# One 128-row tile transposed by TensorE instead of by DMA, two tile loads moved, ten more small products

## The chip, the core and the metric

The kernel runs on one core of a Trainium2 chip. TensorE (PE in the profile; PEld is its weight loads) multiplies, VectorE (DVE), ScalarE (ACT) and GpSimd (POOL) do the elementwise work, and SyncE (SP) issues every DMA of the kernel from one queue. The metric is the device time of one execution in microseconds (us); lower is better.

## The reference, cut to what matters

```python
x = A_x                                   # 1 x 2048 x 640, bf16
xn = layernorm(x)                         # no gain, no bias
# A: 32 heads of 20; phi(u) = [softmax(u w_phi), softmax(-u w_phi)]
q, k, v = split(xn @ wqkv)
kv = phi(k)^T v;  z = sum_s phi(k);  num = phi(q) kv;  den = phi(q) z
a = (num / (den + 1e-6)) @ wo
# B: gated unit, F = 1536
b = (silu(xn @ w1) * (xn @ w3)) @ w2
return x + a + b
```

## The kernel before

The 2048 rows of x are 16 tiles of 128 rows. A tile is loaded with its rows on the partitions (buffer `xin`, printed by the profile as `reg_h`), VectorE and ScalarE work out mean and variance (`ln_stats`, `ln_root`, or `stats` on GpSimd for later tiles), `lx` normalises it in place (line 289), and it is then transposed into `xnT`, which holds the 640 features in five chunks of 128 partitions and all 2048 rows as columns. Every product reads `xnT`. There are two ways to transpose a tile: `by_dma(t)` (line 759) is one DMA transpose issued by SP, and `by_pe(dst, t, ps)` (lines 294 to 304) is five 128x128 transposes on TensorE into the PSUM bank `ps` and two copies by ScalarE, of two and three chunks, into `dst`.

All engines run through one order that is written out by hand, and each of them takes its instructions strictly in that order. The part that the change touches is the opening, lines 764 to 841:

- Tiles 0, 1 and 2 are also transposed before normalisation (`by_pe(xrT, ...)`), so that their products with the v weights (`raw_part`, line 308) can begin while the statistics are made; `raw_scaled` (lines 320 and 325) then multiplies by 1/std.
- For `xnT`, tiles 0, 1 and 3 go by TensorE (lines 780, 790 and 805), tile 2 by DMA (line 795), tiles 4 to 15 by DMA.
- The first two gate and up units work in halves of 256 columns (`glu_half`, line 476): the first half of the gates (lines 810 and 812) needs tiles 0 and 1 alone, then come the v product of tile 3 (`by_token`, line 357) and the first half of the ups, and only the second halves (lines 826 to 829) read tiles 2 and 3. Behind them the third unit (`g2`, line 837, products on line 459) is the first that reads the weight columns 256 to 512, which `ld_glu(256, 512)` loads (line 797).
- SP's queue holds, in order: w1 and w3 columns 0 to 256 and x of tiles 4 and 5; the transpose of tile 2; x of 6 and 7; w1 and w3 columns 256 to 512; x of 8 and 9; x of 10 and 11; the transposes of tiles 4, 5, 6 and 7; x of 12 to 15. A DMA whose data isn't ready holds up everything behind it in this queue.
- `warm(n, cols)` (line 221) multiplies a block of zeros into a PSUM bank that nobody reads.

After the opening come the phi(k) stage with the kv sums, the phi(q) stage, in which gate and up units fill the gaps (`fill`, and `fill_halves` at its step 0, line 719), and the output products (lines 652, 657 and 598). `fill_halves(gate, up)` makes one unit in which the last `gate` and `up` of the five chunks are multiplied as two products of 256 columns in place of one of 512.

At its very end the program branches on a flag (line 998): a general path of two loops, 31 and 55 products long, is skipped, and the last rows are added and stored (`finish`). Every engine executes that branch.

Of the kernel before, what the change touches and what calls it, by code (L numbers as in the profile page):

```python
# [8 lines left out]
P = 128  # L9
# [3 lines left out]
def kernel(  # L13
# [53 lines left out]
    def bank(name, dt=f32):  # L67
        n = 512 if dt == f32 else 1024
        return psum.tile([P, n], dt, name=name, tag="bank")
# [5 lines left out]
    xnT = one.tile([P, KD, S], bf, name="xnT")  # L75
# [69 lines left out]
    def ld(dst, src):  # L145
        nc.sync.dma_start(out=dst, in_=src)
# [9 lines left out]
    with tc.manual_schedule():  # L156
# [6 lines left out]
        def ld_tiles(t, n):  # L163
            ld(
                xin[:, (t // 4) % 3, t % 4 : t % 4 + n],
                x2[t * P : (t + n) * P, :].rearrange("(t p) d -> p t d", p=P),
            )
# [51 lines left out]
        def warm(n, cols=P):  # L219
            for _ in range(n):  # L220
                nc.tensor.matmul(idle[:, 0:cols], nought[:], nought[:, 0:cols])  # L221
# [19 lines left out]
        def ln_stats(*ts):  # L241
            made = []
            for t in ts:
                xt = xin[:, (t // 4) % 3, t % 4, :]
                st = work.tile([P, 2, 6], f32, name="st")
                for i in range(2):
                    nc.vector.bn_stats(out=st[:, i, :], in_=xt[:, i * HD : (i + 1) * HD])  # L247
                made.append(st)
            for t, st in zip(ts, made):
                nc.vector.bn_aggr(out=mv[:, t, :], in_=st[:])  # L250
# [43 lines left out]
        def by_pe(dst, t, ps):  # L294
            xt = xin[:, (t // 4) % 3, t % 4, :]
            for c in range(KD):
                nc.tensor.transpose(  # L297
                    ps[:, c * P : (c + 1) * P], xt[:, c * P : (c + 1) * P], ident[:]
                )
            for c0, c1 in ((0, 2), (2, KD)):  # L300
                nc.scalar.copy(  # L301
                    out=dst[:, c0:c1, t * P : (t + 1) * P],
                    in_=ps[:, c0 * P : c1 * P].rearrange("p (c s) -> p c s", s=P),
                )
# [43 lines left out]
        def tile_of(t):  # L348
            return slice(t * P, (t + 1) * P)
# [104 lines left out]
        def glu_unit(sc, fi, banks=None):  # L454

            gp, up = banks or (bank("gp")[:], bank("up")[:])
            for ps, w in ((gp, w1), (up, w3)):
                for c in range(KD):
                    nc.tensor.matmul(  # L459
                        ps,  # L460
                        w[:, c, fi * P : (fi + 1) * P],
                        xnT[:, c, sc * 512 : (sc + 1) * 512],
                        start=(c == 0),
                        stop=(c == KD - 1),
                    )
            return glu_done(sc, fi, gp, up)

        def glu_done(sc, fi, gp, up):
            th = work.tile([P, 512], f32, name="th")
            nc.scalar.activation(out=th[:], in_=gp, func=AF.Tanh, scale=0.5)  # L470
            return lambda: glu_product(sc, fi, gp, up, th)

        def glu_half(i, w, sc, fi, ps):

            for c in range(KD):
                nc.tensor.matmul(
                    ps[:, i * 256 : (i + 1) * 256],
                    w[:, c, fi * P : (fi + 1) * P],
                    xnT[:, c, sc * 512 + i * 256 : sc * 512 + (i + 1) * 256],
                    start=(c == 0),  # L480
                    stop=(c == KD - 1),
                    skip_group_check=True,
                )
# [101 lines left out]
        def residual(rows):  # L585
            xr = work.tile([P, D], bf, name="xr")
            ld(xr[:], x2[rows, :])
            return xr
# [117 lines left out]
        def fill(n):  # L706
            for _ in range(n):
                glu_unit(*glu.pop(0))()

        def fill_halves(gate, up):  # L710

            sc, fi = glu.pop(0)
            gp, upp = bank("gp")[:], bank("up")[:]
            for ps, w, whole in ((gp, w1, KD - gate), (upp, w3, KD - up)):
                for c in range(KD):
                    n = 1 if c < whole else 2
                    for i in range(n):
                        a, b = i * 512 // n, (i + 1) * 512 // n
                        nc.tensor.matmul(
                            ps[:, a:b],  # L720
                            w[:, c, fi * P : (fi + 1) * P],
                            xnT[:, c, sc * 512 + a : sc * 512 + b],
                            start=(c == 0),
                            stop=(c == KD - 1),
                            skip_group_check=True,
                        )
            glu_done(sc, fi, gp, upp)()
# [8 lines left out]
        def lx(t0, n):  # L736
            if t0 < BY_ROOT:
                nc.vector.reciprocal(out=rstd[:, t0 : t0 + n], in_=ry[:, t0 : t0 + n])
            for t in range(t0, t0 + n):
                ln_x(t)  # L740
# [6 lines left out]
        def two(name):  # L747
            both = pair(name)
            return both[:, 0], both[:, 1]
# [8 lines left out]
        def by_dma(t):  # L758
            nc.sync.dma_start_transpose(out=xnT[:, :, tile_of(t)], in_=xin[:, (t // 4) % 3, t % 4, :])
# [3 lines left out]

        pst = [bank("pst", bf), bank("pst", bf)]
        by_pe(xrT, 0, pst[0])
        warm(4)
        ln_stats(0)
        ln_root(0)
        by_pe(xrT, 1, pst[1])
# [22 lines left out]
        for t in range(3):  # L792
            raw_part(t, 2, vps[t])
        lx(2, 1)
        by_dma(2)
        ld_tiles(6, 2)
        ld_glu(256, 512)
        ld_tiles(8, 2)
        ld_tiles(10, 2)
        lx(3, 1)  # L800
        for t in range(3):
            for c in (3, 4):
# [7 lines left out]
        glu_half(0, w1, sc, fa, ga)  # L810
        gb = bank("gp")[:]
        glu_half(0, w1, sc, fb, gb)
        ln_stats(4, 5)
        ps3 = by_token(tile_of(3), wv, "pv", CH, two("pv"))
        ln_root(4)
# [15 lines left out]
        g1 = glu_done(sc, fb, gb, ub)  # L831
        by_dma(4)
        by_dma(5)
        g0()
        g1()
        lx(6, 2)
# [98 lines left out]
        for t in range(NST + 4):  # L935
            if t < NST:
                phi_unit(t, wqphi, "pq")
            if t < 2:
                kv_unit(turns[t - 2], vaug[:, turns[t - 2]], acc, False, t == 1)
                if t == 1:  # L940
                    kv_done([acc[:, 0], acc[:, 1]])
                    ld(w2, B_w2.rearrange("(c p) d -> p c d", p=P))
            if t < 7:
                (fill_halves(2, 2) if t == 0 else fill(1))
                fill(1)
            for g, c in pieces.get(t, []):
                out_piece(g, c)
            outs = {16: (12,), 19: (13, 14, 15)}.get(t, ())
            for j in outs:
                last = tile_of(j) if j == NST - 1 else None  # L950
                res = out_unit(hT[:, j], tile_of(j % 4), xrs[j], last)
                if j == 13:
                    group_stored(2, 0)
                    group_stored(2, 1)
                if 13 <= j < 15:
                    xrs[j + 1] = residual(tile_of(j + 1))
                if last is None:
                    ld(out2[tile_of(j), :], res[:])
            if 2 <= t < NST + 2:
                r_unit(t - 2)  # L960
            if t < NST:
                phi_transposed(t)
            if 2 <= t < NST + 2:
                o_transposed(t - 2, (t - 2) // 4)
            if t in backs:
                group_back(*backs[t])
            if t in (12, 13):
                group_stored(0, t - 12)
            if t == 17:
                group_stored(1, 0)  # L970
            if 2 <= t < 6:
                x_back(t - 2)
            if 7 <= t < 11:
                x_back(t - 3)
            if 13 <= t < 17:
                x_back(t - 5)
            if t == 15:
                xrs[12] = residual(tile_of(12))
            if t == 17:
                xrs[13] = residual(tile_of(13))  # L980
            if t == 18:
                group_stored(1, 1)
                group_back(2, 0)
                group_back(2, 1)
            if t < 4:
                norm_unit(wqphi, 1, t)
            if t == 4:
                ld(listed[:], norms[:])
                ld(flat, listed[:].rearrange("p g -> (p g)").partition_broadcast(1))
            if t == 10:  # L990
                flag_unit()
            if t == 12:
                ok = nc.values_load(flag[0:1, 0:1], min_val=0, max_val=1)
# [59 lines left out]
```

## Time and profile before

| | |
|---|---|
| median of three runs | 268.84 us (268.24 to 269.27) |
| the profiled execution | 268.56 us, of which 266.9 us are its span from first to last instruction |
| TensorE busy | 261.0 us, 98% of the span |
| VectorE, ScalarE, GpSimd busy | 72%, 42%, 34% |
| granted TensorE clock, mean | 0.998 |
| DMA | 31.41 MB, of which 28 packets are code ("instruction") |

The times of single instructions below are from the profiled execution; its 1.7 us outside the span are not resolved further. Busy time of TensorE is the union of products whose ends are modelled, so a gap in its work is better seen in the starts of products than in the share of busy time.

### The profile page before, as it was taken

To read this page: it belongs to the slowest core of one execution; us is meant where nothing else is said; L and a number is where in the kernel's file an instruction comes from. 1 tells how busy PE (TensorE), PEld (TensorE's weight loads), DVE (VectorE), ACT (ScalarE), POOL (GpSimd) and SP (SyncE) were. 2 spreads that over 40 slices of the span, in tenths; PEclk is the share of its full clock that TensorE was granted. 3 is DMA by queue.
4 is the path that set the end of the run, shared out by engine and by line. 5 is a ranking of instruction groups with operands and counts; after the bars stand their busy time and mean duration, and the time that the engine had idled before them with its cause. 6 is when DMAs were issued, how large, how long until landed. Compare 5 with 4: busy or idle time off the path is not lost.

```text
span 266.9 us, 5027 instructions
## 1 busy us (share of the span) xinstructions
PE 261.0 (98%) x1854; PEld 153.2 (57%) x1880; DVE 193.3 (72%) x356; ACT 113.0 (42%) x347; POOL 90.7 (34%) x83
## 2 busy tenths in 40 slices
PE   8999999999999999999999999999999999999994
PEld 7766475655556555555655555555555555644663
DVE  4899973397876877799888999999699866125121
ACT  5764344746567753366766554423322330000000
POOL 5022620055544444443373333336434543000000
PEclk9999999999999999999999999999999999999999
DMA  6997866976000001500008855563768789552871
GB/s 190 234 259 168 119 122 144 366 133 122 1 2 0 1 3 8 167 2 0 2 0 251 180 120 116 93 133 89 130 153 97 165 200 159 128 116 47 221 209 55
DMA packets 83484, 31.41 MB, mean 118 GB/s; under 512 B 71935, under 2 KB 82047, under 8 KB 83456
## 3 DMA queue, kind: packets, MB, share of 16 engines
q1 hardware_dynamic: 83456, 31.05, 53.5%
q8 instruction: 16, 0.26, 0.4%
q14 instruction: 12, 0.10, 0.1%
HBM read 11.17 MB, written 2.63 MB: 52 GB/s over the span
## 4 chain that ended last, share of the span: by engine, by line
PE 94%; DMA 2%; ACT 1%; issue 1%; SPq 0%; DVE 0%
PE up L459 18%; PE gp L459 18%; PE acc L652 15%; PE pq L357 8%; PE pk L357 8%; PE acc L598 7%; PE pv L357 6%; PE acc L657 6%; DMA w<-in_B_w_dram 2%; PE pr L535 2%; PE pkv L500 2%; PE pf L443 1%; PE idle L221 1%; PE pst L297 1%; ACT xnT L301 0%
## 5 line engine op out<-in xcount | busy, mean ns | idle before, releaser
L423 POOL TENSOR_TENSOR phi<-phi,rk 128x1320 bf16<-128x1320 bf16 x32 | 77.2, 2414 | 108.9 <-DVE rk L422 86.3
L459 PEld LDWEIGHTS <-w 128*128 128x128 bf16 x450 | 42.6, 98 | 47.4 <-DMA w<-in_B_w_dram 0.7
L420 DVE TENSOR_REDUCE sk<-phi 128x66 f32<-128x1320 bf16 x32 | 48.8, 1525 | 19.6 <-ACT phi L386 18.2
L459 PE MATMUL up<-xnT,w 128*128 128x512 bf16 x224 | 55.9, 379 | 0.2
L459 PE MATMUL gp<-xnT,w 128*128 128x512 bf16 x207 | 54.6, 379 | 1.1 <-DMA w<-in_B_w_dram 0.3
L357 PEld LDWEIGHTS <-xnT 128*128 128x128 bf16 x450 | 42.8, 98 | 19.2
L386 ACT ACTIVATE phi<-pq 128x360 bf16<-128x360 f32 (+2 forms) x96 | 24.8, 364 | 42.1 <-issue 31.8
L652 PE MATMUL acc<-reg_h,reg_v 128*128 128x512 bf16 x180 | 41.3, 379 | 0.0
L470 ACT ACTIVATE th<-gp 128x512 f32<-128x512 f32 x48 | 29.2, 610 | 27.0 <-PE gp L459 27.0
L490 DVE SCALAR_TENSOR_TENSOR reg_h<-gs,up 128x512 bf16<-128x512 bf16 x48 | 33.0, 688 | 5.4 <-PE pv L357 0.5
L487 DVE SCALAR_TENSOR_TENSOR gs<-th,gp 128x512 bf16<-128x512 f32 x48 | 31.4, 654 | 4.8 <-ACT th L470 4.8
L386 ACT ACTIVATE phi<-pk 128x360 bf16<-128x360 f32 (+2 forms) x96 | 24.9, 368 | 19.3 <-PE pk L357 19.3
L652 PEld LDWEIGHTS <-reg_v 128*128 128x128 bf16 x180 | 17.4, 98 | 19.1
L357 PE MATMUL pk<-wkphi,xnT 128*128 128x360 bf16 (+1 forms) x160 | 24.3, 299 | 0.0
L357 PE MATMUL pq<-wqphi,xnT 128*128 128x360 bf16 (+1 forms) x160 | 24.3, 299 | 0.0
L422 DVE RECIPROCAL rk<-sk 128x66 f32<-128x66 f32 x32 | 18.1, 566 | 3.2
L357 PE MATMUL pv<-reg_w,xnT 128*128 128x360 bf16 (+1 forms) x130 | 18.6, 299 | 0.0
L607 DVE TENSOR_TENSOR res<-acc,xr 128x320 bf16<-128x320 f32 (+3 forms) x9 | 3.8, 451 | 16.6 <-PE acc L598 10.5
L247 DVE BATCH_NORM_STATS2 st<-reg_h 128x6 f32<-128x320 bf16 x32 | 13.4, 477 | 2.1 <-DMA reg_h<-in_A_x_dram 2.1
L372 ACT CAST reg_v<-pv 128x360 bf16<-128x360 f32 (+2 forms) x39 | 10.6, 347 | 9.7 <-PE pv L357 9.7
L556 DVE TENSOR_TENSOR o__77<-pr,den 128x360 bf16<-128x360 f32 (+1 forms) x32 | 14.2, 486 | 0.6
L660 DVE TENSOR_TENSOR w<-acc,v_raw 128x512 bf16<-128x512 f32 x10 | 6.6, 671 | 10.5 <-issue 6.0
(90 smaller groups left out, 210.8 us busy)
## 6 DMA issues: line engine op xcount, KB each, us to landing
w<-in_B_w_dram SPq DMA_DIRECT2D x2, 1280.0 KB, 6.1
reg_h<-in_A_x_dram SPq DMA_DIRECT2D x6, 320.0 KB, 5.1
reg_v<-in_B_w_dram SPq DMA_DIRECT2D x1, 1920.0 KB, 8.8
out_dram<-w SPq DMA_DIRECT2D x6, 320.0 KB, 2.7
w<-in_B_w_dram SPq DMA_DIRECT2D x4, 320.0 KB, 5.8
reg_w<-in_A_wqkv_dram SPq DMA_DIRECT2D x5, 160.0 KB, 3.6
reg_w<-in_A_wo_dram SPq DMA_DIRECT2D x1, 800.0 KB, 7.5
reg_h<-in_A_x_dram SPq DMA_DIRECT2D x4, 160.0 KB, 3.7
```

The source lines that it names most:

```text
L357: nc.tensor.matmul(ps[i][:, 0 : b - a], xnT[:, c, cols], w[:, c, a:b], start=(c == 0), stop=(c == KD - 1), skip_group_check=True,)
L386: nc.scalar.activation(out=dst[:, c0 : c0 + n, g, 0:k], in_=p.rearrange("p (c f) -> p c f", c=n), func=AF.Exp, scale=1.0 - 2.0 * g,)
L420: nc.vector.reduce_sum(out=sk[:], in_=rows, axis=AX.X)
L422: nc.vector.reciprocal(out=rk[:], in_=sk[:])
L423: nc.gpsimd.tensor_mul(out=rows, in0=rows, in1=rk[:, :, :, None].to_broadcast([P, 2 * NCH, 3, Dh]))
L459: nc.tensor.matmul(ps, w[:, c, fi * P : (fi + 1) * P], xnT[:, c, sc * 512 : (sc + 1) * 512], start=(c == 0), stop=(c == KD - 1),)
L470: nc.scalar.activation(out=th[:], in_=gp, func=AF.Tanh, scale=0.5)
L487: nc.vector.scalar_tensor_tensor(out=gs[:], in0=th[:], scalar=1.0, in1=gp, op0=ALU.add, op1=ALU.mult)
L490: nc.vector.scalar_tensor_tensor(out=hT[:, 4 * sc : 4 * sc + 4, fi, :], in0=gs[:].rearrange("p (t s) -> p t s", t=4), scalar=0.5, in1=up.r ...
L598: nc.tensor.matmul(ps[:, 0 : b - a], rows[j][0], rows[j][1][:, a:b], start=(j == 0), stop=(j == len(rows) - 1),)
L652: nc.tensor.matmul(acc4, w2[:, k, cols], hT[:, 4 * g : 4 * g + 4, k, :], start=(k == 0), stop=False,)
L657: nc.tensor.matmul(acc[:], wo[:, k, cols], oTs[g][:, k, :], start=False, stop=(k == KD - 1),)
```

## The change

Tile 2's `xnT` part is made by TensorE and ScalarE, behind the two first gate halves, and its DMA transpose leaves SP's queue. The load of x for tiles 10 and 11 becomes two loads of one tile, moved in SP's queue behind the transposes of tiles 4 and 5. Ten small products are added without more to compute: eight zero products of 64 columns in place of four of 128 at the start (`warm`), and all five chunks in two halves in place of two of five at step 0 of the phi(q) stage, for gate and for up (three more products each).

```diff
         by_pe(xrT, 0, pst[0])
-        warm(4)
+        warm(8, P // 2)
         ln_stats(0)
...
         lx(2, 1)
-        by_dma(2)
         ld_tiles(6, 2)
         ld_glu(256, 512)
         ld_tiles(8, 2)
-        ld_tiles(10, 2)
         lx(3, 1)
...
         glu_half(0, w1, sc, fb, gb)
+        by_pe(xnT, 2, pst[1])
         ln_stats(4, 5)
         ps3 = by_token(tile_of(3), wv, "pv", CH, two("pv"))
...
         by_dma(4)
         by_dma(5)
+        ld_tiles(10, 1)
+        ld_tiles(11, 1)
         g0()
...
             if t < 7:
-                (fill_halves(2, 2) if t == 0 else fill(1))
+                (fill_halves(5, 5) if t == 0 else fill(1))
                 fill(1)
```

## The prediction

> **What bounds the kernel now.** I read the page first: busy times and the chain that ended last.
>
> ```profile
> PE 261.0 (98%) x1854; PEld 153.2 (57%) x1880; DVE 193.3 (72%) x356; ACT 113.0 (42%) x347; POOL 90.7 (34%) x83
> ...
> PE 94%; DMA 2%; ACT 1%; issue 1%; SPq 0%; DVE 0%
> ```
>
> TensorE is the bound: 94% of the chain is its products. An edit is worth something only where the chain leaves TensorE, so I looked for those places, by the starts of successive products (512 columns step by 0.216 us, 256 by 0.109, a transpose by 0.055). From 17.1 us to the last product at 263.3 I find no step that isn't explained by a record missing from the trace. What is left is the opening, and 3.4 us behind the last product. First the opening, in the chain in order of time:
>
> ```profile
> 10.06 0.57 SPq L759
> ...
> 11.29 5.75 DMA w<-in_B_w_dram
> ...
> 17.10 0.39 PE gp L459
> ```
>
> The third gate unit waits for weight columns 256 to 512; their load waited on SP behind the transpose of tile 2 (line 759). TensorE's own timeline gives the size:
>
> ```profile
> 10.64 0.44 PE L297 MATMUL pst<-ident,reg_h 128*128 128x128 bf16 x5
> 10.91 1.25 PE L476 MATMUL gp<-xnT,w 128*128 128x256 bf16 x10
> 12.01 1.52 PE L357 MATMUL pv<-reg_w,xnT 128*128 128x360 bf16 x10
> ...
> 16.09 0.71 PE L476 MATMUL up<-xnT,w 128*128 128x256 bf16 x5
> 17.10 1.25 PE L459 MATMUL gp<-xnT,w 128*128 128x512 bf16 x4 [0.29 <-DMA w<-in_B_w_dram]
> ```
>
> The last five halves start at 16.09 and take 5 x 0.109 = 0.545, so TensorE could go on at 16.64; it goes on at 17.10. The wait is **0.46 us** (the bracket shows less, because ends are modelled). Now SP's timeline:
>
> ```profile
> 9.31 1.32 SPq L759 DMA_TRANSPOSE xnT<-reg_h  x1
> 10.68 0.57 SPq L146 DMA_DIRECT2D reg_h<-in_A_x_dram  x1
> 11.29 1.53 SPq L146 DMA_DIRECT2D w<-in_B_w_dram  x2
> ...
> 14.72 7.80 SPq L759 DMA_TRANSPOSE xnT<-reg_h  x4
> ```
>
> SP had finished the issue before it at 7.00, so the transpose of tile 2 cost this queue 2.3 us of waiting for the normalised tile and 1.3 us of issuing.
>
> Then the end: the instructions of the branch's line, SP's waits in the last 5 us, and the DMA queues from 262.5 to 266:
>
> ```profile
> L998 PEldq COMPARE_BRANCH  x1: 3244/3244/3244, 262.5 to 262.5; - x1
> ```
>
> ```profile
> SPq L1048 <- PEq L998: 1.1, 1, 1.1
> ```
>
> ```profile
> q8 instruction: 1, 0.02, 1.8%
> ```
>
> The branch takes 45 to 72 ns on the other four engines and 3.24 us on TensorE, from 262.55 to 265.79, and SP's closing waits end on TensorE's instruction behind it (265.91), not on the last store, which is issued at 263.81 and lands 1.8 us later, at 265.63. In that stretch one packet of TensorE's code arrives on q8 (0.26 MB in 16 packets in all: 16 KB each). So the end waits **0.28 us** (265.91 less 265.63) for code.
>
> **The opening, part by part.** *Removed:* SP's transpose of tile 2. The loads of x 6 and 7 go out at about 7.05 instead of 10.68, the two of columns 256 to 512 at about 7.6 and 8.1 instead of 11.29 and 12.30. How early do they land? Best, 5.8 us after issue as now: 13.4. Worst, they queue behind what is under way: the first w3 piece, issued at 6.53, lands 6.3 us later, at 12.8; behind it come x 6 and 7 and w1's piece, 640 KB, at the 213 GB/s that the stretch from 10 to 14 moved: 3.0 us, 15.8; w3's piece at 17.3. TensorE needs them at 16.9 and 18.0 (below). I take the worst, since the transfers are saturated up to 12.8, and it is still early: the wait of 0.46 goes, whole.
>
> *Added on TensorE:* five transposes, 0.27 us by the row at 10.64 (next start 10.91). They are reached at 12.01 and use the bank that ScalarE empties of tile 3 until 11.87, so they don't wait; if ScalarE were later, the v product of tile 3, the up halves and all behind them would wait as long. They are on the path: +0.27. *Added on ScalarE:* two copies, 0.75 us. Its timeline has a hole for them:
>
> ```profile
> 11.12 0.75 ACT L301 COPY xnT<-pst 128x256 bf16<-128x256 bf16 x2 [0.42 <-PE pst L297]
> ...
> 11.76 0.96 ACT L325 ACTIVATE v_raw<-pv,rstd 128x360 f32<-128x360 f32 x2
> 13.53 0.48 ACT L265 ACTIVATE ry<-mv,eps 128x1 f32<-128x1 f32 x2 [0.81 <-DVE mv L250]
> ```
>
> The copies go from 12.72 to 13.47, in 0.81 us of waiting for VectorE. Without that cover the root of tile 4 and its transpose would be up to 0.75 later; that transpose lands at 20.4 and is read at 21.4, which hides this too. The second halves read tile 2 from 14.73 on: 1.2 us to spare.
>
> *Moved:* x of 10 and 11 on SP. Two issues of about 0.45 us stand where SP is free from 18.0 to 20.0, waiting for tile 6; a load here lands in 3.6 to 5.9 us, so by 24, and tile 10's statistics start behind 27. Nothing. One transpose and 320 KB less ahead of the transposes of tiles 4 to 7 can only help; they aren't late now.
>
> *Ten small products:* eight of 64 columns for four of 128 in the first 6 us, where 128 columns still step by 0.107 us: line 221's forty of 64 took 2.15 us, 54 ns each, so 8 x 54 against 4 x 107: nothing. Six more by halving: 2 x 0.109 against 0.216 is 2 to 3 ns each, +0.015 us.
>
> Opening: -0.46 + 0.27 + 0.015 = **-0.17 us**, bounds -0.46 (if the transposes cost nothing) to +0.29 (if the whole wait stayed).
>
> **The end.** The change issues 15 more TensorE products, each with a weight load, ahead of the branch. Code comes in by equal blocks, so what a block ends on is shifted. The windows between q8's packets (206.0, 223.5, 242.3; the next at 263.3) show the rhythm; the fourth column group is PEld:
>
> ```profile
> 223.50:242.25 18.75, 18.64 (x118) 10.08 (x119) 4.73 (x12) 0.00 (x0) 1.06 (x1) 1.00 0.57 107
> 242.25:262.55 20.30, 20.25 (x135) 12.68 (x135) 5.90 (x14) 0.00 (x0) 0.00 (x0) 1.00 0.62 162
> ```
>
> A block lasted 119, 123 and 133 loads; 135 had gone when the branch began. The refill that the branch waits for was thus due just there. With 15 pairs more ahead it falls 15 pairs earlier, and the products before the branch (160 columns) step by 0.07 us: 1.05 us. The branch would end near 264.7, before the last store lands: the end gains the 0.28, not more, since the store is late next. Bounds: 0 (the refill is asked for by the branch itself) to -0.28.
>
> [...]
>
> **Sum.** -0.17 - 0.28 = -0.45: 268.56 to 268.1 for the profiled execution. The median of the three runs is 0.28 above that one, so I say 268.4.
>
> **Rivals.**
> *The end doesn't move.* For it: 135 is hardly over 133, so the edge may lie behind the branch even with 15 pairs more. Then the opening alone counts: 268.84 - 0.17 = 268.7.
>
> [...]
>
> *The early loads get in the way.* Four loads more from 7.0 on share with x 4 and 5 (landing at 11.6, read at 11.71) and w3's first piece (12.8, now read at 13.64). If all in flight shared evenly, the 800 KB or so outstanding at 9 would take twice as long: w3 lands at about 14.8, TensorE waits 1.2, and with the gains that is +0.7: 269.5. Against it: ten loads issued 0.45 us apart land in the order of issue. [...]
>
> **How the numbers follow.** The forecast 0.46; the end unmoved 0.22; loads in the way 0.12; two refills 0.14; 0.06 for a gain that I don't see, such as a wait at 17.1 that is longer in other executions. Half a per cent, 1.3 us, is about what a measurement of this kernel can tell from no change. Forecast, unmoved end and most of the third case lie within it: 0.72. Slower: two refills and the far end of the third, 0.17. Faster: the 0.06 and some scatter of the runs (they spread over 1.0 us), 0.11. The range takes in forecast, unmoved end and loads in the way, with that scatter: 267.5 to 270.0.
>
> **What would show it.** Right: the third gate unit starts without a wait near 16.9; w's loads issued before 9; ScalarE's copies of tile 2 done by 13.5; a branch on TensorE near 2.2 us that nobody waits for, and the last store closing the span. Wrong: a wait ahead of the up halves at 13.6 (loads in the way), a q8 packet both before and inside a branch of over 5 us (two refills), or any new step in TensorE's products behind 22 us.

## The result, and the profile after

The changed kernel takes 269.07 us (median of 22 executions, 268.44 to 269.83); the kernel before takes 268.06 (22, 267.20 to 269.63). The ratio is 1.004, 95% interval 1.003 to 1.005: 1.0 us slower, where 0.45 us less was forecast. Over these 22 executions the median of before is 0.8 below that of the three shown ahead of the prediction. That 269.07 lies inside the forecast range of 267.5 to 270.0 is luck: the upper part of the range was there for early loads in the way and for scatter, not for what happened.

The profiled execution of the changed kernel takes 268.92 us with a span of 267.2. In its opening the edits do what was forecast. TensorE's timeline, as shown of before:

```profile
11.51 0.44 PE L297 MATMUL pst<-ident,reg_h 128*128 128x128 bf16 x5
11.79 1.52 PE L357 MATMUL pv<-reg_w,xnT 128*128 128x360 bf16 x10
...
15.88 0.71 PE L476 MATMUL up<-xnT,w 128*128 128x256 bf16 x5
16.64 1.03 PE L459 MATMUL gp<-xnT,w 128*128 128x512 bf16 x4
```

The five transposes of tile 2 take 0.28 (11.51 to 11.79), and the third gate unit follows with no wait. (One record of it is missing; its first weights load at 16.32, before the last halves are done.) SP's timeline has the reason, the loads of w at 7.55 instead of 11.29, and ScalarE's has the two copies in their hole:

```profile
7.55 1.73 SPq L146 DMA_DIRECT2D w<-in_B_w_dram  x2
```

```profile
11.26 0.96 ACT L325 ACTIVATE v_raw<-pv,rstd 128x360 f32<-128x360 f32 x2
12.09 0.77 ACT L301 COPY xnT<-pst 128x256 bf16<-128x256 bf16 x2
13.03 0.48 ACT L265 ACTIVATE ry<-mv,eps 128x1 f32<-128x1 f32 x2 [0.16 <-DVE mv L250]
```

The last store is issued at 263.14, 0.67 earlier than before (263.81). Most of the 0.67 can't be put down to the change: the first gate half starts 0.49 earlier (10.42 against 10.91), ahead of the five transposes, and this start varies between profiles of one kernel (10.69 and 10.79 in two more of before, 11.03 in another of the changed kernel). The span is nevertheless 0.35 longer, so the loss in this pair of profiles is behind that issue. The branch's line (now 999), SP's waits from 262 us on, and the DMA queues and issues from the last store's issue on (263.1 to 265.3):

```profile
L999 PEldq COMPARE_BRANCH  x1: 1295/1295/1295, 261.9 to 261.9; - x1
```

```profile
SPq L1049 <- DMA out_dram<-res: 2.1, 1, 2.1
```

```profile
q8 instruction: 1, 0.02, 3.8%
...
out_dram<-res SPq DMA_DIRECT2D x1, 64.0 KB, 3.2
```

The branch is shorter, 1.3 us for 3.24, and nothing waits for it any more. But SP now waits 2.1 us for the last store, which lands 3.2 us after its issue where it took 1.8. In the same stretch there is a packet of TensorE's code: it starts at 263.91, 0.73 after the branch ends, and takes 1.32 us, to 265.23. The trace has the sixteen completions of the store: fifteen are in by 264.67, 1.53 after its issue, and the sixteenth comes at 266.31. Eight of its 128 packets of 512 bytes, one sixteenth, go out only from 265.22 on, when the code is through. In the profile of before this second refill starts at 266.53, when everything has landed (window 266.5:266.6):

```profile
q8 instruction: 1, 0.02, 66.3%
```

I call it the second refill; the first is the one that the branch waits for, whose packet ran from 260.81 to 261.74 here and from 263.34 to 264.36 in the profile of before.

I call "the end" the time from the issue of the last store to the end of the span. Before: 266.86 - 263.81 = 3.05 us. After: 267.21 - 263.14 = 4.07.

### The profile page after: what moved, and what is told of

It reads as the page before. It is cut to its first block, busy times and chain, and to the rows that moved or that the text cites. A ratio compares the mean times of both kernels' runs of the same rounds, so it can differ in the third digit from the quotient of the medians.

```text
span 267.2 us, 5059 instructions
## 1 busy us (share of the span) xinstructions
PE 260.3 (97%) x1869; PEld 153.9 (58%) x1895; DVE 193.1 (72%) x356; ACT 113.6 (43%) x349; POOL 90.6 (34%) x83
## 4 chain that ended last, share of the span: by engine, by line
PE 96%; DMA 1%; issue 1%; SPq 0%; DVE 0%
PE up L459 18%; PE gp L459 18%; PE acc L652 15%; PE pq L357 8%; PE pk L357 8%; PE acc L598 7%; PE pv L357 7%; PE acc L657 6%; PE pr L535 2%; PE pkv L500 2%; DMA reg_w<-in_A_wqkv_dram 1%; PE pf L443 1%; PE pv L308 1%; PE up L476 1%; PE gp L476 1%
```

## The experiments

The theory: the code refill that starts behind TensorE's branch (0.73 us after its end above) holds one sixteenth of the last store, and it is the number of product pairs (a weight load and a product) ahead of the branch that sets where this refill falls. The first rival is that the opening's edits cost something; the second, that the ten products cost time where they stand. The runs were made on three chips, four runs on each; every ratio is to executions of before on the same chip.

**The opening alone (e1_opening), 5 pairs more than before.**

```diff
  (the changed kernel, with)
-        warm(8, P // 2)
+        warm(4)
-                (fill_halves(5, 5) if t == 0 else fill(1))
+                (fill_halves(2, 2) if t == 0 else fill(1))
```

> The opening's edits alone, without the ten small products: 5 product pairs more than before ahead of the branch instead of 15. Theory (the code refill behind TensorE's branch runs into the last store): the refill that the branch waits for comes only about 0.4 us earlier than before, the branch takes about 2.9 us, the refill behind it falls about 2.4 us after the last store's issue, when its packets are through, so that the store lands within 1.8 us: about 267.5, 0.5 below before. Rival 1 (the opening's edits cost somewhere in the middle): 268.5 or more. Rival 2 (the ten products cost time where they stand): about 267.8, with the last store's landing unchanged by them.

Measured: 267.68 against 267.69, ratio 0.9999 (0.9987 to 1.0011). The branch takes 2.64 (2.9 expected), the second refill starts 2.12 after the last store's issue, and the store lands within 1.5; its end is 2.45. So the tail is as the theory says, but the 0.5 below before isn't there. Two more profiles of before follow below, because one is too few to compare with; none of them is from this chip, so why the gain is missing here stays open.

**The ten products alone (e2_ten), 10 pairs.** The kernel before with the two edits of the diff on `warm` and `fill_halves`.

> The ten small products alone, on the kernel before. Theory (refill): 10 pairs, the branch takes about 2.5 us, the refill behind it starts about 1.9 us after the last store's issue, behind the store's packets; the store lands within 1.8 us and nothing waits for the branch: about 267.8, 0.2 to 0.3 below before. Rival 2 (the products cost time where they stand): 269.0, all of the loss. Rival 1: as before, 268.06.

Measured: 268.82 against 267.69, ratio 1.0047 (1.0030 to 1.0064): all of the loss and more. The branch takes 1.375, not 2.5: ten pairs shift the first refill by more than the 0.07 us per pair that I took, so the second starts 0.84 after the store's issue, while the store is under way:

```profile
L998 PEldq COMPARE_BRANCH  x1: 1375/1375/1375, 261.8 to 261.8; - x1
```

```profile
out_dram<-res SPq DMA_DIRECT2D x1, 64.0 KB, 3.1
```

Fifteen completions are in by 1.54, the last comes at 3.10. By the time alone this is what the second rival expected; by the place of the loss it isn't: the ten products' own stages are no longer than before (from the first weight load of tile 4's v product to the last weight load of the kernel 242.04 us, against 242.03, 242.07 and 242.03 in the three profiles of before; and the first gate half, behind the zero products, starts at 10.48, where it starts at 10.69 to 10.91 in those).

**Ten and twenty products more (e3_more10, e4_more20), 25 and 35 pairs.**

```diff
  (the changed kernel, with)
-                (fill_halves(5, 5) if t == 0 else fill(1))
+                (fill_halves(5, 5) if t < 2 else fill(1))     # e4_more20: t < 3
```

> The changed kernel with ten more halved products at step 1 of the phi(q) stage: 25 pairs more than before ahead of the branch. Theory (refill): the target's code is there before the branch, which takes under 0.3 us; the refill behind it starts before the last store's packets and holds the store before it; the last one lands about 1.8 us after its issue: about 267.3 to 267.6, 1.5 below the changed kernel. Rival 2 (products cost time where they stand): 269.1 or more.

> The changed kernel with twenty more halved products (steps 1 and 2): 35 pairs. Theory (refill): as with 25 pairs, branch under 0.1 us, refill behind it well before the last store: 267.3 to 267.6. Rival 2: 269.2 or more.

Measured: 268.58, ratio 1.0041 (1.0028 to 1.0054), and 268.26, ratio 1.0029 (1.0018 to 1.0041), against 267.69. In both the first refill had been through for 2.4 and 3.3 us, and the branch takes 0.38 (under 0.3 and under 0.1 expected):

```profile
L999 PEldq COMPARE_BRANCH  x1: 384/384/384, 262.3 to 262.3; - x1
```

Neither comes down to the 267.3 to 267.6 expected. In their tails I see one reason: the refill behind the branch can't come early enough. The branch begins 1.26 before the store's issue in every kernel here, so even this refill starts about 0.1 before the issue and still holds the store's last sixteenth, to 2.31 and 1.93 instead of 1.53. It holds it less than with 10 or 15 pairs, and the kernel with more products is the faster of the two, against the second rival. Against the opening alone, on the same chip, they take 0.90 and 0.58 more, of which their ends are 0.76 and 0.37.

**Before, the changed kernel, and before with 15 pairs, on one chip (e5_before, e7_after, e6_before15).** The last has the ten products and `fill_halves(5, 0)` at step 1.

> The kernel before once more, for its profile and times on the chip of the runs beside it. Theory (the profile shown before is a typical one): third gate unit near 17.1 us, branch 3.2 us, span near 266.9, 268.0 to 268.6. Rival (that profile caught a late start of the opening and a long refill; most executions have less of both): first products of line 459 near 16.4 and span near 266.0, with a time equal to the opening's edits alone, 267.7.

> The kernel before with 15 more product pairs (the ten, and five more by halving at step 1 of the phi(q) stage) and none of the opening's edits: as many ahead of the branch as the changed kernel has. Theory (the count of pairs sets where the refill falls, and it holds the last store): last store's landing 3.0 to 3.2 us behind its issue with 15 of its 16 completions at 1.5; as slow as the changed kernel to 0.3 us, 268.8 to 269.1. Rival (the loss is the opening's, with by_pe or the moved loads): as before.

> The changed kernel once more beside them. Theory: last store lands 3.0 to 3.2 us behind its issue; 1.0 above before; against e6_before15, which differs in the opening alone, it tells what the opening is worth: -0.2 by the prediction's sum, 0 or more by the rival that the opening gives nothing.

Measured, against 268.09: before once more 267.99; before with 15 pairs 268.94, ratio 1.0036 (1.0021 to 1.0050); the changed kernel 269.23, ratio 1.0043 (1.0029 to 1.0058), with its store landing after 2.9. The profile of e5_before lies between its two expectations: a branch of 3.12, but a third gate unit at 16.81 without a wait there and a span of 266.5. With equally many pairs, the kernel without any of the opening's edits is as slow as the changed one to 0.3 us. The profiled execution of e6_before15 is the fastest of its twelve (267.98): there the first refill came early, and the second, 0.03 after the store's issue, held the store to 2.12 only, short of the 3.0 to 3.2 expected:

```profile
L998 PEldq COMPARE_BRANCH  x1: 555/555/555, 262.0 to 262.0; - x1
```

```profile
out_dram<-res SPq DMA_DIRECT2D x1, 64.0 KB, 2.1
```

So that the loss varies with the place of the refill from execution to execution is argued: the twelve run from 267.98 to 270.38, and no profile shows one of the slower ones of this kernel.

**One block more (e8_period), 133 pairs, 128 more than the opening alone has.** From one packet on q8 to the next the trace of before has 97 to 154 weight loads, 127 on the mean of the 14 stretches up to the refill that the branch waits for, so by that count 128 pairs are about one block (the code of one packet).

```diff
  (the changed kernel, with)
-                (fill_halves(5, 5) if t == 0 else fill(1))
-                fill(1)
+                (fill_halves(4, 4) if t == 6 else fill_halves(5, 5))
+                (fill_halves(5, 5) if t < 6 else fill(1))
```

> [...] Theory (only the place within a block counts): the tail is that of the opening alone, with the branch near 2.6 us, the last store landing within 1.6 us of its issue and the refill behind it; the products cost 118 x 2.5 ns = 0.3 us: 0.3 above the opening alone and 1.0 below the changed kernel, about 268.0. Rival (more code or more products cost, steadily): 269.5 or more, above the changed kernel.

Measured: 267.99, ratio 1.0001 (0.9987 to 1.0015) against 268.09. This kernel has 17 packets on q8 where the changed one has 16: the added products of TensorE brought one packet more. That a block is 128 pairs exactly isn't shown. With 118 products more than the changed kernel it is 1.2 us faster, on one chip. Its tail is that of the opening alone: branch 2.27 (2.6 expected), second refill 1.75 after the store's issue, landing 1.54, end 2.43. The 118 products themselves cost 0.30 us, 2.5 ns each as expected (242.34 against 242.04 us from tile 4's v product to the last weight load). This is the run that tells the count within a block from the count itself; since 5 and 6 pairs (below) give the same tail, it fixes the period to a few pairs only:

```profile
L999 PEldq COMPARE_BRANCH  x1: 2269/2269/2269, 262.8 to 262.8; - x1
```

```profile
out_dram<-res SPq DMA_DIRECT2D x1, 64.0 KB, 1.5
```

```profile
q8 instruction: 17, 0.28, 0.4%
```

**Six products alone, another order of SP's queue, before and the opening again (e9_six, e10_queue, e11_before, e12_opening).** e9_six is before with `fill_halves(5, 5)` alone, 6 pairs; e11_before and e12_opening are before and e1_opening again; e10_queue is

```diff
  (e9_six, with)
+        ld_glu(256, 512)
         by_dma(2)
         ld_tiles(6, 2)
-        ld_glu(256, 512)
```

> The kernel before with six of the ten small products alone (all five chunks halved at step 0 of the phi(q) stage): 6 pairs ahead of the branch. Theory (place of the refill): branch 2.5 to 2.7 us, the refill behind it 2.0 to 2.2 us after the last store's issue and behind its packets, the store lands within 1.6; end 2.45 us behind the last store's issue, 0.5 less than before: 267.5. Rival (any pairs added cost, as ten and fifteen did): 268.4 to 268.6.

> As the one with six products, and in SP's queue the load of weight columns 256 to 512 stands ahead of tile 2's DMA transpose instead of behind it; nothing moves to TensorE. Theory (the opening's edits pay five transposes, 0.27 us, for a wait of as much): the wait at the third gate unit goes and nothing is paid: from the first gate half to the v product of tile 4 9.9 us instead of 10.1 to 10.3; 0.2 to 0.3 below the one with six alone, about 267.3. Rival (the transpose of tile 2 now lands late behind 640 KB and the second halves wait for it): a wait ahead of them at 14.5, 268 or more.

> The kernel before again, a third profile, on the chip of the runs beside it. Theory: end 2.9 to 3.1 us behind the last store's issue, TensorE's branch last; first gate half to v product of tile 4 between 9.9 and 10.35, changing from execution to execution. 268.0.

> The opening's edits alone again, beside a profile of before on the same chip. Theory (the opening nets 0, and the tail gains 0.5 by the place of the refill): 10.16 us from first gate half to the v product of tile 4, end 2.45 behind the last store's issue, 0.4 to 0.5 below before. Rival (nothing is gained, as measured on the other chip): as before, with a tail above 2.9.

Measured, against 268.07: six products 267.64, ratio 0.9984 (0.9975 to 0.9994); the opening alone 267.74, ratio 0.9982 (0.9972 to 0.9992); before again 267.99; the other order 268.99, ratio 1.0033 (1.0021 to 1.0045). Six pairs and five pairs gain here, ten lose on their chip. The expected tail of 2.45 is met (2.44 and 2.42; the branches are shorter than expected, 2.20 for 2.5 to 2.7 in e9_six). The gain is 0.3 to 0.4 rather than 0.5, and a reason is at hand: before is not always at 3.05. In e11_before the refill came early enough for an end of 2.46, where 2.9 to 3.1 was expected.

The other order fell to its rival. TensorE's timeline has the wait ahead of the second halves, for the DMA transpose of tile 2, now behind two weight loads:

```profile
13.56 1.25 PE L476 MATMUL up<-xnT,w 128*128 128x256 bf16 x10
15.45 0.71 PE L476 MATMUL gp<-xnT,w 128*128 128x256 bf16 x5 [0.63 <-DMA xnT<-reg_h]
```

By starts of products it is 0.80 us (1.09 after 13.56 would be 14.65). So in this order the early weight loads aren't to be had with the DMA transpose behind them. Its tail is that of six pairs. Of the 1.3 us between its profile and that of e9_six the opening has 0.58, a first gate half that starts later 0.46, and a longer wait for tile 12's transpose near 39 us (on this wait, see below) 0.28; that the last two come from the order isn't shown.

| pairs | kernel | second refill starts after the store's issue | store lands (15 of 16, all) | end | ratio to before |
|---|---|---|---|---|---|
| 0 | before, 3 profiles | 2.73, 2.60, 2.14 | 1.5 to 2.0, 1.5 to 2.0 | 3.05, 2.92, 2.46 | 1 |
| 5 | e1, e12 | 2.12, 1.68 | 1.5, 1.5 | 2.45, 2.42 | 0.9999, 0.9982 |
| 6 | e9 | 1.86 | 1.5, 1.5 | 2.44 | 0.9984 |
| 6 | e10 (other queue order) | 1.89 | 1.5, 1.5 | 2.44 | 1.0033 |
| 10 | e2 | 0.84 | 1.5, 3.1 | 4.00 | 1.0047 |
| 15 | after, e7 | 0.77, 0.66 | 1.5, 3.2 and 2.9 | 4.07, 3.79 | 1.004, 1.0043 |
| 15 | e6 (its fastest execution) | 0.03 | 1.5, 2.1 | 3.02 | 1.0036 |
| 25 | e3 | -0.13 | 1.5, 2.3 | 3.21 | 1.0041 |
| 35 | e4 | -0.08 | 1.5, 1.9 | 2.82 | 1.0029 |
| 133 | e8 | 1.75 | 1.5, 1.5 | 2.43 | 1.0001 |

The rows hang together by two steps of nearly constant length. In the twelve profiles in which TensorE's branch waits, it ends 1.39 to 1.46 us after the packet of the first refill does; and the second refill starts 0.72 to 0.79 us after the branch's end in twelve of the fourteen (0.92 in e9_six, 1.15 in e10_queue). The other code packet near the last store, an 8 KB one of q14, starts within 0.13 us of its issue in all fourteen, whether the store is held or not, so it doesn't make the difference.

## Why the prediction was wrong, step by step

**"The end gains the 0.28, not more, since the store is late next"**: this is the step that failed. Its first half held: 15 pairs do put the branch's refill earlier, by about 2 us instead of 1.05 (the branch falls from 3.24 to 1.3), and nobody waits for the branch. But I took the store's landing of 1.8 us as fixed. The refill that follows the branch moved with it, from behind the store into the middle of it, and the store landed after 3.17. What replaces -0.28 is +1.02 by the two profiles (end 3.05 to 4.07). The measured +1.0 is of that size; over three profiles of before and two of the changed kernel the ends differ by 1.1 on the mean (2.81 and 3.93).

The profile of before had two lines of warning that I didn't read. The windows of q8 gave a second packet, at 266.53, behind the branch (shown above). And the store before the last one had been held in just this way by the first refill (263.34 to 264.36): issued at 262.21, it had fifteen completions by 1.61 and the last at 3.26, while the smaller store behind it took 1.8:

```profile
out_dram<-res SPq DMA_DIRECT2D x1, 96.0 KB, 3.3
```

How the refill holds the store is read from the times: the refill is one packet of 16 KB (263.91 to 265.23), and eight of the store's 128 packets, one sixteenth, go out only from 265.22 on, while the other fifteen completions are in by 1.53 as in the kernels whose store isn't held. The trace doesn't name the DMA engine of a packet; that the held sixteenth shares one with the refill is the author's inference.

**The sum of the opening, -0.17**: the edits did what was said, but one term was mis-sized and one wait wasn't foreseen. The five transposes cost 0.28 as forecast. The wait that they were to remove was 0.46 in the one profile that I had. Between the first gate half and tile 4's v product it is 0.46, 0.40, 0.08, 0.18, 0.22 and 0 in six profiles of kernels with the old opening and the old queue order (before three times, e2, e9, e6; 9.88 us without a wait), and none in the seven with the new one (9.88 and 0.28 for the transposes, 10.16 in all seven); the 0.40 and the 0.22 are ahead of the up halves, for the first piece of w3. The mean is 0.22, so up to there the edits cost 0.06. Further on there is what the prediction called a sign of being wrong, a new step in TensorE's products: near 38 us the weight loads of tile 12's v product wait for that tile's DMA transpose (e7_after, window 30:45):

```profile
PEld L357 <- DMA xnT<-reg_h: 0.4, 1, 0.4
```

By the starts of products this is worth 0.12 to 0.25 us in five of the seven profiles with the new opening, 0.04 and 0.09 in two of the six with the old, and nothing in the profiles of before and after compared above. On the mean it is 0.13 against 0.02. So on the mean of these profiles the opening costs 0.16 us where -0.17 was forecast. The times of kernels that differ in it and have about as many pairs fit that (267.74 and 267.64 for e12 and e9, 269.23 and 268.94 for e7 and e6), though differences of this size are hardly clear of the scatter. Why tile 12's transpose is late isn't settled.

**The ten products** cost next to nothing where they stand, as forecast, and most of the loss by their number. In e8 118 more of the same kind cost 0.30 us, which its shorter end (2.43) makes up for: its time is that of before.

**The rivals.** "The end doesn't move" is out. "Two refills" expected a q8 packet both before and inside a branch of over 5 us. No run shows such a branch: the longest takes 3.24 us (before), and that of the changed kernel 1.3, with a packet ahead of it (260.81 to 261.74) and none inside. Slower by about a microsecond came all the same, by another way: a second refill that holds a store and not TensorE. "The early loads get in the way" isn't seen in the changed kernel's profile: x of 4 and 5 lands at 11.1 and w3's first piece at 12.1, earlier than before. In e7 the last piece of the v weights, issued long before the loads that were moved, lands at 9.4, and TensorE stands idle 0.75, by the times for it (the profile names no releaser); over all profiles the first weight load of the gate halves is at 10.66 us on the mean with the new opening (seven) and at 10.67 with the old (six), so nothing of it remains on the mean. Of the transposes of tile 2 on TensorE and the moved loads of x 10 and 11 neither was run by itself; they are together in all the kernels with the new opening, and no wait of TensorE in their profiles is for the x of tile 10 or 11.

**A version that beats both.** The opening alone, and before with six halved products, take 0.18% and 0.16% less than before (intervals above, one chip), by an end that is 2.4 in every profile of theirs (three). On another chip the opening alone showed no gain, so this is little. The three ends of before (3.05, 2.92, 2.46) suggest that it is a gain of steadiness; more profiles would have to show it.

Not settled: why a pair shifts the refill by more than the 0.07 us of its product (10 pairs took 1.3 to 1.9 us off the branch, by which of the three profiles of before one takes), and why the first refill comes at places 0.6 us apart, by the branch's start, in the profiles of before.

## What to carry to other kernels

When a program ends in a branch, look at what the code refills do to the last transfers, and not only at how long the branch takes: list the packets of the code queue beside the issue and landing of each late store. Here a change that only added instructions moved those refills (e2_ten: 1.1 us slower), so a difference of a microsecond may have nothing to do with what the change is for; a control with the same number of instructions, or with one block more, tells the two apart. And a wait of half a microsecond in one profile should be read in several before it is booked as a gain.

## What the runs showed of the hardware that was not expected

A refill of 16 KB of code is one packet and took 0.9 to 2.1 us in these profiles. Where it fell into the 64 KB store at the end, one sixteenth of the store landed 0.4 to 1.6 us after the other fifteen, which were in by 1.5 us. Behind TensorE's taken branch another refill started, 0.72 to 0.79 us after the branch's end in twelve of fourteen profiles, also in the two whose branch had not waited for code; in the profile of before its packet was still under way when the span ended (266.53 and 1.06, against 266.86), so nothing in the kernel needed it. A branch on TensorE whose refill had been through for 2.4 and 3.3 us took 0.38 us, against 0.05 to 0.07 on the other engines.
